# Attention, experts and a second FFN on one core: w_out's loads move to ACT's queue, stage one's operands are requested and summed at other places, two small steps are reordered

## The chip, the cores and the metric

The kernel runs on one core of a Trainium2 chip. The metric is the device time of one execution in microseconds (us); lower is better. The engines named below are PE (TensorE), DVE (VectorE), ACT (ScalarE), POOL (GpSimd) and SP (SyncE, which here only issues transfers). "PEld" is the loading of PE's weights.

## The reference

Three layers follow one another; `x` and `state` go in, 2304 rows of 512 numbers come out.

```python
def reference(**kw):
    attn_out = _attn_ref(x, state)              # 4 x 8 heads, 512 + 32 rows each, 64 wide
    x = attn_out.transpose(0, 2, 1, 3).reshape(2304 - 128, 512)   # rows of one token
    x = _moe_ref(x=x, **moe)                    # top-1 of 8 experts: relu(x @ w1[e]) @ w2[e], gated, capped
    return _moe2_ref(x=x, **moe2)
def _moe2_ref(x, w_in, w_out):
    h = x @ w_in                                # 512 -> 2048
    g = h * np.clip(h + 3.0, 0.0, 6.0) / 6.0
    return (g @ w_out).astype(np.float32)       # 2048 -> 512
```

## The kernel before, in words

After the attention (to about 73 us) come the experts: tiles of 256 tokens, one expert each, numbered s. For a tile, `xt` transposes the gathered rows on PE (L765) and splits them into a high part (ACT, L759) and a low part (DVE, L760). `gate` computes the gate's weight (DVE L775 to L782, ACT L778), `row` spreads it over the partitions (PE L788, ACT L789). Then `m1` (L797) and `m2` (L808) multiply by the expert's weights. Every float32 product is three matmuls of split halves (high by high, low by high, high by low). A tile whose expert differs from that of the tile ahead enters a branch (`tc.If`, `split`) in which its weights are split; all engines that have work in it evaluate the branch.

The **middle stage** (`mm3`, L1125, 264.5 to 440.7 us) is the first product of the second FFN: 7 chunks c of 256 tokens by 16 column blocks m. A block is 12 matmuls of 128x256 into one of eight PSUM banks taken in turn; ACT computes u (L1107), DVE g (L1108; four buffers of g), and SP writes g into `g_all` in DRAM (L1135). In the shadow of chunks 1 and later a generator, `wo_make`, prepares w_out a step at a time: `out_load` (L937) fetches half a block of w_out (512 KB, tile `st`, two buffers), DVE joins its 64-bit words into float32 (`bits`, L924, L926, L928, tile `wsrc`), POOL forms four differences (L1278), ACT and DVE split them (L1289, L1291). Blocks 6 and 7 are made first and put away in DRAM by four writes each (`wo_d`, L1298, on SP); `wo_back` (L1305, on POOL) fetches them during the next stage. In the steps of a block the load of each half stands one half ahead of its use.

The last product, g by w_out, uses Strassen and Winograd's seven products (`PRODS`) of 2 by 2 blocks. In **stage one** (L1469, 440.6 to 478.0 us) all seven sums of chunk 0 grow side by side over eight inner blocks, here called pairs j = 0 to 7; each takes 21 matmuls. For each j, `a_load(j)` brings four quarter tiles of g from `g_all` by two transfers of 128 KB on SP (L1338), `a_make(j)` forms four sums of 128x128 on POOL (L1343) and then calls `parts`: a cast on ACT (L1328) and a subtraction on DVE (L1329). The raw tiles come from a ring of six slots. Chunks 1 to 6 follow (L1489) with 128x1024 sums on POOL (L1399).

Each engine works through its own instructions in the order in which the code calls them; SP, ACT and POOL issue transfers in that same order.

Of the kernel before, what the change touches and what calls it, by code (L numbers as in the profile page):

```python
# [594 lines left out]
def full(ctx, tc, x, state, w_gate, w1, w2, capacity, w_in, w_out, out, dbg=None):  # L595
    nc = tc.nc
    V, A, G, T = nc.vector, nc.scalar, nc.gpsimd, nc.tensor
# [118 lines left out]
    w64o = w_out.bitcast(I32)  # L716
# [20 lines left out]
    def loads(which, fl, pool=None, tag=None):  # L737
        return {k: load(which, fl[1], k, fl[0], pool=pool, tag=tag) for k in (0, 2, 1, 3)}
# [8 lines left out]
    def split(which, raws, pool=(1,)):  # L747
        for k in (0, 2, 1, 3):
            split1(which, k, raws[k], pool)
# [184 lines left out]

    def out_load(m):
        st = cv.tile([128, 1024], I32, name="st")
        nc.sync.dma_start(out=st, in_=w64o[128 * m:128 * m + 128, :])  # L937
        return st

    def vload(m):  # L940
# [49 lines left out]
    def gate(xg, n=2):  # L990
        idt = ew.tile([128, 2], F32, name="idt", bufs=5)
        return idt, gate_into(xg, ew.tile([128, 2, E], F32, name="lg"), ew.tile([128, 2, 2], F32, name="mx", bufs=4), idt, n)

    def row(gv):
        gB = ew.tile([128, 256], F32, name="gB", bufs=1)
        gate_row(pT.tile([128, 256], F32, name="pgb", tag="T"), gv, gB)
        return gB

    def xt(xg):
        xT = [ew.tile([128, 4, 256], F32R, name=f"xt{h}", bufs=1) for h in "hl"]  # L1000
        for t in range(2):
            xt_into(xg[:, t], p3.tile([128, 512], F32, name="pxt", tag="3"), *(v[:, :, 128 * t:128 * t + 128] for v in xT))
        return xT
# [146 lines left out]
    vload(0)  # L1150
    vload(1)
    ids, gBs = {}, {}
    xT = {N0: xt(xg[N0])}
    ids[N0], gv = gate(xg.pop(N0))
    with tc.If(fl[N0][0] != 0):  # L1155
        split(0, r0.pop(N0))
    r1[N0] = loads(1, fl[N0])
    ft, pr, pe, pg, pid, pth, py = {}, {}, {}, {}, {}, {}, {}
    pend = sorted(PAIRS.items())
# [15 lines left out]
    for s in range(N0, NF):  # L1175
        last = s + 1 == NF
        p, n = PAIRS.get(s), PAIRS.get(s + 1)
        if p is not None:
            hp = p_m1(pth.pop(p), pr.pop(p))
            pr[p] = p_loads(1, pe[p], range(4))  # L1180

        def after0():
            with tc.If(fl[s][0] != 0):
                split(1, r1.pop(s))
            if last:
                ft[0] = fetch_c(0)
            else:
                r0[s + 1] = loads(0, fl[s + 1])
            if s == N0:
                gBs[s] = row(gv)  # L1190
            for q in [q for q in py if py[q] is not None]:
                p_y(py[q], pid[q][0], slice(256 * NF + 128 * q, 256 * NF + 128 * q + 128))
                py[q] = None

        def after1():
            if last:
                prep(0)
                for t in range(2):
                    ft[0][1](t)
                ft[1] = fetch_c(1)  # L1200
            steps(1)

        def between():
            if not last:
                ids[s + 1], gvs[0] = gate(xg.pop(s + 1))
            if n is not None:
                pid[n] = gate(pg.pop(n), 1)
            steps(1)
            if last:
                prep(2)  # L1210

        gvs = [None]
        hT = m1(xT.pop(s), {0: after0, 1: after1})
        if last:
            for t in range(2):
                ft[1][1](t)
            prep(1)
        else:
            xT[s + 1] = xt(xg[s + 1])
            if n is not None:  # L1220
                pth[n] = p_xt(pg[n])
            if s + 2 < NF:
                xg[s + 2] = gather(lrow(s + 2))
            with tc.If(fl[s + 1][0] != 0):
                split(0, r0.pop(s + 1))
            r1[s + 1] = loads(1, fl[s + 1])
            if s + 2 < NF:
                fl[s + 2] = flags(s + 2)
        if p is not None:
            hp = p_ht(hp)  # L1230
        m2(hT, ids.pop(s), gBs.pop(s), slice(256 * s, 256 * s + 256), between)
        if not last:
            gBs[s + 1] = row(gvs[0])
        steps(1)
        if p is not None:
            py[p] = p_m2(hp, pr.pop(p), pid[p][1])
        if pend and pend[0][0] == s + 2:
            p_begin()
# [87 lines left out]
    def parts(a):  # L1326
        hi, lo = htile(), htile()
        A.copy(hi, a)  # L1328
        V.tensor_tensor(out=lo, in0=a, in1=hi.bitcast(F32), op=ALU.subtract)  # L1329
        return hi, lo  # L1330
# [3 lines left out]
    def a_load(j):  # L1334
        AO[j] = a = rtile()
        for h in range(2):
            m = 8 * h + j
            nc.sync.dma_start(out=a[:, 2 * h:2 * h + 2].rearrange("p n j -> p (n j)"), in_=g_all[0:128, 256 * m:256 * m + 256])  # L1338

    def a_make(j):  # L1340
        a = AO[j]
        for o, x, z, op in ((4, 1, 3, ALU.add), (6, 0, 1, ALU.subtract), (5, 4, 0, ALU.subtract), (7, 2, 5, ALU.subtract)):
            G.tensor_tensor(out=a[:, o], in0=a[:, x], in1=a[:, z], op=op)  # L1343
        AO[j] = parts(a)


    PRODS = ((3, 6), (0, 0), (4, 3), (6, 5), (5, 4), (2, 1), (7, 2))
# [82 lines left out]
    for c in range(NCS):  # L1430
        for m in range(0 if c else 2, 16):
            if c == 0 and m in (2, 4, 6):
                r = slice(3 * m - 6, min(3 * m, 17))
                nc.sync.dma_start(out=out.rearrange("(p r) d -> p r d", r=17)[:, r], in_=zt[:, 0:DM].unsqueeze(1).broadcast_to([128, r.stop - r.start, DM]))
            mm3(m, c)
            if c == 0:
                advance(2)
                if m < 7:
                    prep(m + 1)
            else:  # L1440
                next(wg_, None)
                if m % 5:
                    next(wg_, None)
            if 0 < c < NCS - 1:
                if m == 2:
                    ft[c + 1] = fetch_c(c + 1)
                if m in (7, 10):
                    ft[c + 1][1](m // 8)
            if c == NCS - 1:
                if m == 7:  # L1450
                    a_load(0)
                    a_load(1)
                if m in (9, 11):
                    a_make(m // 2 - 4)
    for _ in wg_:
        pass

# [3 lines left out]
    fids = [ft[c][0][2] for c in range(NCS)]  # L1461
    acc = [bank(n) for n in range(7)]
    for j in range(8):
        if j + 2 < 8:
            a_load(j + 2)
        hl = AO.pop(j)
        for (x, z), ps in zip(PRODS, acc):
            for n, (l, r) in enumerate(SPLIT):
                T.matmul(ps, hl[l][:, x], WO[j][z][r], start=j == 0 and n == 0, stop=j == 7 and n == 2)  # L1469
        if j + 2 < 8:  # L1470
            a_make(j + 2)
        if NWA + j < 8:
            wo_back(NWA + j)
        if j > 2:
            q_step(1, j - 4)
# [132 lines left out]
```

## Time and profile before

| | us |
|---|---|
| median of 3 runs | 606.24 (605.2 to 608.19) |
| the profiled execution | 608.2 |
| its span in the trace | 606.2 |
| PE busy in the span | 554.9 (92%) |
| DVE, ACT, POOL busy | 365.8, 233.1, 216.9 |

The span is the time from the first to the last recorded instruction; 2.0 us of the execution lie outside it. Busy time of PE is the union of its matmuls; the time in which no matmul runs is 51.3 us.

### The profile page before, as it was taken

The page shows a single profiled execution, that of the slowest core. Times are in us where ns is not written, and L with a number is a line of the kernel's source. Part 1 is how long each engine was busy: PE and PEld are TensorE (multiplying, and loading weights), DVE is VectorE, ACT ScalarE, POOL GpSimd, SP SyncE. Part 2 cuts the span into 40 slices and gives each one's busy share as a digit, 9 for nine tenths or more (in the row PEclk, how much of TensorE's full clock was granted, in tenths as well). Part 3 has the DMA queues.
Part 4 walks back from the last instruction along what each step waited for, and adds up shares of the span by engine and source line. Part 5 has one row for each costly group of instructions (what it writes and reads, how often), then busy time and mean ns, then how long its engine had stood idle before and what let it go on. Part 6 is the DMA issues. An engine that isn't in the chain of part 4 may idle for free. (4 is left out here: it accounts for less than half of the span.)

```text
span 606.2 us, 12079 instructions
## 1 busy us (share of the span) xinstructions
PE 554.9 (92%) x4478; PEld 507.0 (84%) x4478; DVE 365.8 (60%) x730; ACT 233.1 (38%) x416; POOL 216.9 (36%) x257
## 2 busy tenths in 40 slices
PE   6997898999999999999988798999967899999995
PEld 3665688886968696999988798999966799999995
DVE  5888884355625573563454667665233958878851
ACT  4877640143214150434333444445332534433320
POOL 4436434110501010026101212220247668587841
PEclk9999799799999999999999799999989799999998
DMA  6744612989789774248676574653378334543410
GB/s 138 165 169 161 236 57 79 328 318 303 268 284 359 256 268 140 89 161 308 212 259 217 192 222 144 200 159 130 97 221 282 104 105 139 157 128 120 134 57 29
DMA packets 97906, 112.08 MB, mean 185 GB/s; under 512 B 25809, under 2 KB 74961, under 8 KB 97330
## 3 DMA queue, kind: packets, MB, share of 16 engines
q1 hardware_dynamic: 94178, 100.13, 51.0%
q0 software_dynamic: 3392, 11.05, 5.3%
q8 instruction: 37, 0.61, 0.4%
q14 instruction: 27, 0.22, 0.1%
q10 hardware_dynamic: 272, 0.07, 0.0%
HBM read 89.10 MB, written 34.84 MB: 204 GB/s over the span
## 5 line engine op out<-in xcount | busy, mean ns | idle before, releaser
L1125 PE MATMUL p<-yTh,wh 128*128 128x256 f32 x448 | 114.4, 288 | 9.0 <-DVE g L1108 7.2
L1329 DVE TENSOR_TENSOR ga<-ga 128x1024 fp32r<-128x1024 f32 x50 | 90.5, 1829 | 44.3 <-ACT ga L1328 44.2
L1125 PE MATMUL p<-yTl,wh 128*128 128x256 f32 x448 | 113.4, 283 | 2.0 <-DVE yTl L912 2.0
L1125 PEld LDWEIGHTS p<-yTh,wh 128*128 128x128 f32 x448 | 85.2, 190 | 10.0 <-DVE g L1108 7.8
L1125 PEld LDWEIGHTS p<-yTl,wh 128*128 128x128 f32 x448 | 85.8, 192 | 2.6 <-DVE yTl L912 2.6
L1328 ACT CAST ga<-ga 128x1024 fp32r<-128x1024 f32 x50 | 51.8, 1048 | 87.9 <-POOL ga L1399 34.5
L1107 ACT ACTIVATE u<-p,b 128x256 f32<-128x256 f32 x110 | 51.0, 474 | 81.2 <-DVE g L1108 52.1
L1125 PE MATMUL p<-yTh,wl 128*128 128x256 f32 x448 | 72.1, 283 | 0.0
L1399 POOL TENSOR_TENSOR ga<-ga 128x1024 f32<-128x1024 f32 x24 | 64.4, 2706 | 10.9 <-DMA ga<-g_all 10.7
L1108 DVE SCALAR_TENSOR_TENSOR g<-u,p 128x256 f32<-128x256 f32 x110 | 44.4, 416 | 34.9 <-ACT u L1107 24.5
L1125 PEld LDWEIGHTS p<-yTh,wl 128*128 128x128 f32 x448 | 61.9, 190 | 0.0
L797 PE MATMUL pm<-xth,w1h 128*128 128x256 f32 x160 | 47.0, 294 | 3.8 <-ACTq L1155 3.8
L797 PE MATMUL pm<-xth,w1l 128*128 128x256 f32 x160 | 46.2, 289 | 0.0
L797 PE MATMUL pm<-xtl,w1h 128*128 128x256 f32 x160 | 46.1, 288 | 0.0
L808 PE MATMUL pm<-hth,w2h 128*128 128x256 f32 x160 | 45.1, 282 | 0.2
L808 PE MATMUL pm<-hth,w2l 128*128 128x256 f32 x160 | 44.8, 280 | 0.0
L808 PE MATMUL pm<-htl,w2h 128*128 128x256 f32 x160 | 44.7, 279 | 0.0
L800 DVE SCALAR_TENSOR_TENSOR htl<-pm,hth 128x512 fp32r<-128x512 f32 x20 | 13.5, 687 | 46.7 <-ACT hth L799 23.7
L797 PEld LDWEIGHTS pm<-xth,w1h 128*128 128x128 f32 x160 | 31.2, 195 | 7.3 <-ACTq L1155 4.0
L1278 POOL TENSOR_TENSOR wt<-wsrc 128x256 f32<-128x256 f32 x16 | 13.1, 816 | 64.6 <-DVE wsrc L928 57.5
L1355 POOL DMA_INDIRECT out_dram<-o,fid x14 | 22.5, 1610 | 35.2 <-issue 14.5
L962 POOL TENSOR_TENSOR wl<-v,wh 128x1024 fp32r<-128x1024 f32 x6 | 15.0, 2530 | 49.1 <-ACT wh L961 49.1
(448 smaller groups left out, 1447.7 us busy)
## 6 DMA issues: line engine op xcount, KB each, us to landing
raw<-in_moe_w_dram SPq DMA_DIRECT2D x80, 512.0 KB
g_all<-g SPq DMA_DIRECT2D x110, 128.0 KB
ga<-g_all SPq DMA_DIRECT2D x24, 512.0 KB
st<-in_moe_w_in_dram SPq DMA_DIRECT2D x16, 512.0 KB
st<-in_moe_w_out_dram SPq DMA_DIRECT2D x16, 512.0 KB
x_rows<-xrow SPq DMA_DIRECT2D x4, 1072.0 KB
xb<-in_x_dram SPq DMA_DIRECT2D x32, 128.0 KB
yg<-y_pad SPq DMA_DIRECT2D x14, 258.0 KB
```

The source lines that it names most:

```text
L797: T.matmul(ps[:, j], W1[l][k][:, ls], xT[r][:, k], start=k == 0 and i == 0, stop=k == 3 and i == 2)
L800: V.scalar_tensor_tensor(out=hl, in0=ps, scalar=0.0, in1=hh.bitcast(F32), op0=ALU.max, op1=ALU.subtract)
L808: T.matmul(ps[:, j], W2[l][k // 2][:, k % 2, ls], hT[k // 2][r][:, k % 2], start=k == 0 and i == 0, stop=k == 7 and i == 2)
L962: (V if j in (0, 2) else G).tensor_tensor(out=wl, in0=v, in1=wh.bitcast(F32), op=ALU.subtract)
L1107: A.activation(out=u, in_=ps, func=AF.Relu, bias=b3)
L1108: V.scalar_tensor_tensor(out=g, in0=u, scalar=6.0, in1=ps, op0=ALU.min, op1=ALU.mult)
L1125: T.matmul(pv, l[:, 512 * q + 128 * k:512 * q + 128 * k + 128], r[:, :, 128 * k:128 * k + 128], start=n == 0, stop=n == 11)
L1278: G.tensor_tensor(out=t[:, o], in0=x, in1=z, op=ALU.subtract)
L1328: A.copy(hi, a)
L1329: V.tensor_tensor(out=lo, in0=a, in1=hi.bitcast(F32), op=ALU.subtract)
L1355: G.indirect_dma_start(out=out, out_offset=bass.IndirectOffsetOnAxis(ap=fid[:, t:t + 1], axis=0), in_=o, in_offset=None, bounds_check=B * ...
L1399: G.tensor_tensor(out=QS[c, o], in0=QS[c, x], in1=QS[c, z], op=op)
```

## The change

It has four parts. (1) `out_load` issues its 16 transfers on ACT's queue instead of SP's. (2) For the first tile of the experts' loop, the branch that splits its weights stands ahead of the tile's transposes and gate instead of behind them. (3) `row` of each later tile moves from the end of the `m2` ahead of it into its own `m1`, after the first quarter (`after0`). (4) In stage one the loads of pairs 0 to 3 are requested at m = 7, 8, 9, 10 of the last chunk (before: pairs 0 and 1, both at m = 7); `a_make` is cut into `a_sums` and `a_parts`; the sums of pairs 3 and 4 are formed on DVE, the others on POOL as before; and for each j the load of pair j + 4, the parts of j + 2 and the sums of j + 3 are called ahead of j's matmuls (before: the load of j + 2 ahead, sums and parts of j + 2 behind).

```diff
     def out_load(m):
         st = cv.tile([128, 1024], I32, name="st")
-        nc.sync.dma_start(out=st, in_=w64o[128 * m:128 * m + 128, :])
+        nc.scalar.dma_start(out=st, in_=w64o[128 * m:128 * m + 128, :])
         return st
...
-    xT = {N0: xt(xg[N0])}
-    ids[N0], gv = gate(xg.pop(N0))
     with tc.If(fl[N0][0] != 0):
         split(0, r0.pop(N0))
+    xT = {N0: xt(xg[N0])}
+    gvs = {}
+    ids[N0], gvs[N0] = gate(xg.pop(N0))
...
-            if s == N0:
-                gBs[s] = row(gv)
+            gBs[s] = row(gvs.pop(s))
...
-        if not last:
-            gBs[s + 1] = row(gvs[0])
...
-    def a_make(j):
-        a = AO[j]
+    def a_sums(j):
+        a, eng = AO[j], V if j in (3, 4) else G
         for o, x, z, op in ((4, 1, 3, ALU.add), (6, 0, 1, ALU.subtract), (5, 4, 0, ALU.subtract), (7, 2, 5, ALU.subtract)):
-            G.tensor_tensor(out=a[:, o], in0=a[:, x], in1=a[:, z], op=op)
-        AO[j] = parts(a)
+            eng.tensor_tensor(out=a[:, o], in0=a[:, x], in1=a[:, z], op=op)
+
+    def a_parts(j):
+        AO[j] = parts(AO[j])
...
             if c == NCS - 1:
-                if m == 7:
-                    a_load(0)
-                    a_load(1)
-                if m in (9, 11):
-                    a_make(m // 2 - 4)
+                if m in (7, 8, 9, 10):
+                    a_load(m - 7)
+                if m in (9, 11, 13):
+                    a_sums(m // 2 - 4)
+                if m in (10, 12):
+                    a_parts(m // 2 - 5)
...
     for j in range(8):
+        if j + 4 < 8:
+            a_load(j + 4)
         if j + 2 < 8:
-            a_load(j + 2)
+            a_parts(j + 2)
+        if j + 3 < 8:
+            a_sums(j + 3)
         hl = AO.pop(j)
         for (x, z), ps in zip(PRODS, acc):
             for n, (l, r) in enumerate(SPLIT):
                 T.matmul(ps, hl[l][:, x], WO[j][z][r], start=j == 0 and n == 0, stop=j == 7 and n == 2)
-        if j + 2 < 8:
-            a_make(j + 2)
```

Lines of the kernel after shift by up to three: its L1335 is L1338 of before, L1340 is L1343, L1326 is L1329, L1286 is L1289.

PE's order at the start of the experts' loop, as a difference (L1155 and L1153 are the same branch, L765 are the first tile's transposes):

```order
+L1153 COMPARE_AND_BRANCH
+L1153 UNCONDITIONAL_BRANCH x2
 L765 MATMUL pxt<-identk,xg 128x128 x8
-L1155 COMPARE_AND_BRANCH
-L1155 UNCONDITIONAL_BRANCH x2
 L797 MATMUL pm_1785<-xth,w1h_93 128x256
```

The branch now stands ahead of the transposes, and the same on ACT, DVE and POOL.

SP's queue of before in the middle stage, where the first block of w_out is put away and the loads of the next one follow:

```order
L1135 DMA g_all<-g 128x256 x7
L1298 DMA wo_d<-wo6h 128x1024
L1298 DMA wo_d<-wo6l 128x1024
L1298 DMA wo_d<-wo6bh 128x768
L1298 DMA wo_d<-wo6bl 128x768
L937 DMA st<-in_moe_w_out_dram 128x1024
L1135 DMA g_all<-g 128x256 x2
L937 DMA st<-in_moe_w_out_dram 128x1024
```

ACT's order of the change at the same place (L1286 are casts of w_out, L1107 the activations of blocks, L911 the cast of the next chunk):

```order
L1286 CAST wo6bh<-wsrc 128x512
L1107 ACTIVATE u<-p_4180,b_82 128x256
L937 DMA st<-in_moe_w_out_dram 128x1024
L1107 ACTIVATE u<-p_4207,b_82 128x256
L911 CAST yTh_4046<-yg 128x512
L1107 ACTIVATE u<-p_4229,b_82 128x256
L937 DMA st<-in_moe_w_out_dram 128x1024
L1107 ACTIVATE u<-p_4251,b_82 128x256
```

The two loads no longer stand behind the four writes of `wo_d`, nor behind writes of g; they stand between activations, and the writes stay on SP.

DVE's order of the change in stage one (L1326 are the subtractions of `parts`, L1340 the sums of `a_sums`):

```order
L1326 TENSOR_TENSOR ga<-ga 128x1024
L1340 TENSOR_TENSOR ga<-ga 128x128 x4
L1326 TENSOR_TENSOR ga<-ga 128x1024
L1340 TENSOR_TENSOR ga<-ga 128x128 x4
L1326 TENSOR_TENSOR ga<-ga 128x1024 x7
```

They are, in turn, the low part of pair 2, the sums of 3, the low part of 3, the sums of 4, and then the low parts of 4 to 7 and of chunk 1's first operands. Before, DVE had nine subtractions in a row here and no sum; on POOL the twelve sums that stay behind `wo_back`'s issues are now those of pairs 5, 6 and 7 alone.

SP's order of the change at the same place (L1394 are chunk 1's loads):

```order
L1335 DMA ga<-g_all 128x256 x2
L1135 DMA g_all<-g 128x256 x5
L1335 DMA ga<-g_all 128x256 x8
L1394 DMA ga<-g_all 128x8x128 x24
```

The first row is the load of pair 3; the five writes are those of the last blocks of g, and the loads of pairs 4 to 7 stand right behind them. Before, the loads of pairs 2 to 5 stood behind the last eight writes, and those of 6 and 7 behind loads of chunk 1.

## Rows read from the trace of the kernel before

**Rows 1.** Page, part 1: engine, busy us (share of the span) xinstructions.
```profile
PE 554.9 (92%) x4478; PEld 507.0 (84%) x4478; DVE 365.8 (60%) x730; ACT 233.1 (38%) x416; POOL 216.9 (36%) x257
```

**Rows 2.** Windows table: stretch, length, busy us of each engine, clock, DMA share, GB/s.
```profile
300.00:350.00 50.00, 42.37 (x330) 41.40 (x329) 26.96 (x60) 18.72 (x39) 9.29 (x12) 0.93 0.66 228
...
350.00:400.00 50.00, 46.59 (x385) 45.99 (x384) 33.35 (x74) 23.78 (x50) 11.55 (x15) 1.00 0.55 176
...
440.00:478.00 38.00, 26.95 (x177) 24.73 (x176) 16.98 (x14) 13.54 (x17) 24.76 (x35) 0.87 0.64 201
...
478.00:599.00 121.00, 119.74 (x1008) 119.37 (x1007) 89.73 (x88) 40.53 (x43) 78.00 (x34) 1.00 0.41 120
```

**Rows 3.** Timeline of PE: start, length, instruction, [idle before it <- releaser].
```profile
107.47 0.58 PE L797 MATMUL pm<-xth,w1h 128*128 128x256 f32 x1 [3.80 <-ACTq L1155]
...
136.88 0.43 PE L788 MATMUL pgb<-identk,mx 128*128 128x128 f32 x2 [0.72 <-DVE lg L775]
...
318.25 0.39 PE L1125 MATMUL p<-yTh,wh 128*128 128x256 f32 x1 [1.83 <-DVE g L1108]
...
337.08 0.58 PE L1125 MATMUL p<-yTh,wh 128*128 128x256 f32 x1 [5.14 <-DVE g L1108]
...
471.23 0.58 PE L1469 MATMUL po<-wo7h,ga 128*128 128x256 f32 x1 [2.42 <-ACT ga L1328]
```

**Rows 4.** Timeline of DVE at the first tile of the experts.
```profile
105.34 1.29 DVE L760 TENSOR_TENSOR xtl<-pxt,xth 128x512 fp32r<-128x512 f32 x2 [0.43 <-DVE xb L812]
```

**Rows 5.** Waits: engine, tile, line <- releaser: us in total, times, longest.
```profile
DVE wsrc L924 <- DMA st<-in_moe_w_out_dram: 29.0, 8, 7.2
...
DVE g L1108 <- DMA g_all<-g: 10.3, 5, 5.0
```

**Rows 6.** Timeline of SP's queue in the middle stage.
```profile
310.39 1.02 SPq L937 DMA_DIRECT2D st<-in_moe_w_out_dram  x1
...
328.87 1.33 SPq L937 DMA_DIRECT2D st<-in_moe_w_out_dram  x1
```

**Rows 7.** Timeline of ACT in the middle stage.
```profile
305.07 0.48 ACT L1107 ACTIVATE u<-p,b 128x256 f32<-128x256 f32 x1
...
324.52 0.84 ACT L1107 ACTIVATE u<-p,b 128x256 f32<-128x256 f32 x2 [0.47 <-DVE g L1108]
```

**Rows 8.** Timeline of DVE in the middle stage.
```profile
316.71 0.43 DVE L924 TENSOR_SCALAR wsrc<-st 128x512 int32<-128x512 int32 x1 [6.76 <-DMA st<-in_moe_w_out_dram]
...
335.55 0.43 DVE L924 TENSOR_SCALAR wsrc<-st 128x512 int32<-128x512 int32 x1 [7.17 <-DMA st<-in_moe_w_out_dram]
```

**Rows 9.** Timeline of POOL in stage one.
```profile
447.14 1.81 POOL L1343 TENSOR_TENSOR ga<-ga 128x128 f32<-128x128 f32 x4 [7.65 <-DMA ga<-g_all]
...
455.29 7.53 POOL L1343 TENSOR_TENSOR ga<-ga 128x128 f32<-128x128 f32 x12
...
468.29 1.81 POOL L1343 TENSOR_TENSOR ga<-ga 128x128 f32<-128x128 f32 x4 [3.10 <-DMA ga<-g_all]
```

**Rows 10.** Timeline of SP's queue around stage one.
```profile
444.12 3.74 SPq L1338 DMA_DIRECT2D ga<-g_all  x8
...
462.53 0.92 SPq L1338 DMA_DIRECT2D ga<-g_all  x2
```

**Rows 11.** Page, part 5: costliest groups, busy us, mean ns of one.
```profile
L1328 ACT CAST ga<-ga 128x1024 fp32r<-128x1024 f32 x50 | 51.8, 1048 | 87.9 <-POOL ga L1399 34.5
...
L1108 DVE SCALAR_TENSOR_TENSOR g<-u,p 128x256 f32<-128x256 f32 x110 | 44.4, 416 | 34.9 <-ACT u L1107 24.5
```

**Rows 12.** Timeline of DVE in stage one.
```profile
437.95 1.23 DVE L1329 TENSOR_TENSOR ga<-ga 128x1024 fp32r<-128x1024 f32 x1 [4.89 <-ACT ga L1328]
...
442.76 0.79 DVE L1108 SCALAR_TENSOR_TENSOR g<-u,p 128x256 f32<-128x256 f32 x2 [0.27 <-ACT u L1107]
...
463.93 2.34 DVE L1329 TENSOR_TENSOR ga<-ga 128x1024 fp32r<-128x1024 f32 x1 [1.43 <-ACT ga L1328]
```

**Rows 13.** DMA issues: transfer, queue, count, KB each, median us to landing.
```profile
wo6bh<-wo_d POOLq DMA_DIRECT2D x1, 384.0 KB, 8.9
```

More of the change, by code (lines that the diff above doesn't have):

```diff
@@ L1204, in between @@
             if not last:
-                ids[s + 1], gvs[0] = gate(xg.pop(s + 1))
+                ids[s + 1], gvs[s + 1] = gate(xg.pop(s + 1))
             if n is not None:
@@ L1210, in between @@
                 prep(2)
-        gvs = [None]
         hT = m1(xT.pop(s), {0: after0, 1: after1})
```

## The prediction

> **What bounds the kernel now.** The page's first part comes first: PE is busy for 554.9 of 606.2 us [rows 1], so 51.3 us without a matmul are what a change of order can win; no other engine is near its limit. The table of windows says where they lie. In the last stretch, 478 to 599 us, 1008 matmuls take 119.74 us of busy PE, 0.1188 us each, at a granted clock of 1.00 [rows 2]. At that pace 50 us hold 421 matmuls; the stretch 300 to 350 has 330, so 91 are missing, or 10.8 us. Its idle time is 50 - 42.37 = 7.6 us; the other 3.2 us are matmuls run at the lower of the clock's two levels, 1.2 instead of 2.4 GHz; the mean clock of 0.93 shows them, in a stretch whose other feature is that PE stood idle. The stretch 350 to 400 misses 36 matmuls, 4.3 us. Stage one (440 to 478) misses 320 - 177 = 143, or 17.0 us: 11.0 idle, 6.0 at the lower clock (mean 0.87). So 32 of the losses lie in the stretches that the change touches. The timeline of PE names what ended the waits: in the middle stage DVE's g (1.83 and 5.14 us), in stage one the operands' parts, at the start of the experts the branch (3.80), and at 136.88 the gate's row (0.72) [rows 3].
>
> **Start and rows.** Before, PE sat 3.80 us until the branch (the wait that ended last is ACT's queue at L1155) and began at 107.47. With the branch ahead, what PE needs is xtl, and DVE has it at 105.34 + 1.29 = 106.63 [rows 4]. That is 0.8 us earlier; I take 0.6, since the branch itself still costs something where it now stands. Bounds: 0 if the branch costs as much ahead of the transposes, and 1.5 if PE can start on the first half of xtl. The moved `row` removes the wait of 0.72 at the second tile; a quarter of `m1` (24 matmuls, 2.9 us) now covers the gate's last steps on DVE and ACT. I take 0.7, bounds 0 and 1. Together **1.3 us**.
>
> **w_out's loads.** DVE waits 29.0 us in eight waits for `st` [rows 5]; the two longest are 6.76 (to 316.71) and 7.17 (to 335.55) [rows 8]. Everything behind the waiting conversion on DVE is late by it: the g of the blocks, so the PSUM banks, so PE once its lead of eight banks (11.4 us at 1.43 a block) is used up; that is where 1.83 and 5.14 come from. The two late loads are issued by SP at 310.39 and 328.87 [rows 6], each just behind four writes of w_out. On ACT the first stands behind the activation that began at 305.07, so at about 305.6, the second behind the first of the pair begun at 324.52, so at about 325 [rows 7]: 4.8 and 3.9 us earlier, and now ahead of the writes' bytes on the transfer engines instead of behind them. The transfers took 316.71 - 310.39 = 6.3 and 6.7 us from issue to use. If they take as long again, the waits shrink to about 2.0 and 3.3; as they run ahead of the writes, I expect less. A wait of 2 to 3 us is below PE's lead, so all of 1.83 goes and of 5.14 at least 3.9. With the idle time goes most of the lower clock behind it. Of the 10.8 us lost in 300 to 350 I count 9 back, of the 4.3 in 350 to 400, where DVE's waits for `st` are short and the load is issued at about the same time by either engine, 1. **10 us**; bounds 5 (the second wait keeps its transfer time and the clock stays low behind it) and 14 (nearly all of 15.1).
>
> The cost of it: sixteen issues on ACT between activations, at most the 1.33 us that the longer of SP's took [rows 6], 21 us in all. ACT is busy 18.72 of 50 us there [rows 2], so they lie beside PE. The second load of each pair also waits on ACT until DVE has converted the tile that lies in its buffer; behind it stand the activations, and behind those g and PE. DVE's conversion stands just ahead, so I expect a hold of about 1 us, covered by the lead of eight banks.
>
> **Stage one.** 168 matmuls at 0.1188 are 20.0 us; the stage took 37. Before, only pairs 0 and 1 were ready; the loads of 2 to 5 stood behind the last eight writes of g and were issued at 444.12 [rows 10], POOL's first sum came at 447.14 [rows 9], and every pair then paid in turn: four sums on POOL (1.81 alone, 7.53 / 3 = 2.51 in the row of twelve), a cast of 1.05 [rows 11] and a subtraction of 1.23 [rows 12], with eight issues of `wo_back` among the sums. The last load went out at 462.53, once a ring slot was free, and was used at 468.29, 5.76 us later [rows 9, 10]; PE waited 2.42 for that pair's cast alone [rows 3].
>
> Now I count from T, the start of the stage, with 2.49 us a pair. Pairs 0 to 3 are loaded 7 to 13 us before T, the sums of 0 to 2 and the parts of 0 and 1 done in the last blocks. The parts of 2 stand behind the last u on ACT and the last g on DVE. Before, the last g ended at 442.76 + 0.79 = 443.55 [rows 12], 3 us into the stage; now DVE has no other work ahead of it, so I take T + 2.5, the cast from about T + 2 to 3.1, the subtraction to T + 4.3; wanted at 5.0. The four sums on DVE are not in the trace. Between 128x256 (0.416, [rows 11]) and 128x1024 (1.23) the slope is 1.06 ns a column, so 128x128 would be 0.28, four of them 1.1 us; bounds: 4 x 0.416 = 1.7 above, and below 4 x (1.23 / 8) = 0.6. I take 1.1. Pair 3: T + 4.3, sums 1.1, cast 1.05, subtraction 1.23: T + 7.7, wanted at 7.5. Pair 4's load is issued behind the last writes of g, about T + 4.4; it is used 3.0 us later if it goes like that of 444.12, 5.8 if like that of 462.53. Then 3.4 us of sums, cast and subtraction: T + 10.8 to 13.6, wanted at 10.2, so PE waits 0.6 to 3.4. For 5 to 7 POOL needs at most 2.51 us each and PE 2.49, so nothing grows from there. `wo_back`'s eight transfers can be issued within the stage's first 5 us, without sums between them, and land 8.9 us later [rows 13], by T + 14; wanted from T + 15 on. With one or two us at the lower clock the stage takes 22 to 26 us. Of 17.0 lost I count 13 back: **13 us**; bounds 6 and 16.
>
> DVE's sums also meet POOL's. The row at 463.93 shows a subtraction of 2.34 beside a POOL sum of 128x1024, that of 437.95 one of 1.23 beside POOL's sums of 128x128 [rows 12]; so beside small sums I add nothing. The Trainium skill ("SBUF — State Buffer", the section on SBUF's two separate sides) has a DVE operation with two SBUF inputs and a GpSimd operation that reads SBUF lock one shared port pair, the second standing still for the whole of the first. The row of 463.93 agrees, that of 437.95 does not show it; by the rule each of DVE's eight sums could wait for one of POOL's, some 0.5 us each by [rows 9], and the sum here would be 21 instead of 24.
>
> **The sum.** 1.3 + 10 + 13 = 24.3 us. From the profiled execution's 608.2 (span 606.2 and 2.0 around it) that gives 583.9; it lies 2.0 above the median of 606.24, from which it gives 581.9. I predict **583**.
>
> **The rivals.** (a) The w_out loads land no sooner: only the issue moves, while the transfer engines are full with the same writes, so DVE waits until the same time. For it: 6.3 and 6.7 us from issue to use at both places, much above the 3.0 of the load at 444.12. Against it: the new issue lies ahead of the writes. Then 14.3 us are won: 592 to 594. The Trainium skill ("DMA: Bandwidth & Descriptors", the section that issuing engines are not separate DMA queues) speaks for this rival: transfers of all engines run on the same 16 engines, and another issuer saves only the issuing. By that rule rival (a) is the forecast; here the issue itself stood behind other issues, which is what its saving is. (b) Stage one stays bound by transfers: the loads of 4 to 7 now run beside both of `wo_back`'s groups, and take the 8.9 us of those [rows 13] instead of 3 to 6. Pair 4 then comes 4 to 6 us later: 587 to 590. (c) Writes of g land late behind `wo_d`'s, and g's four buffers run out; DVE waited 10.3 us for them in all [rows 5]. It would keep half of the middle stage's gain: 588. (d) Slower: ACT, holding a w_out load until its buffer is free, holds the activations. In eight blocks each hold beyond PE's lead costs PE the rest. To use up 24 us of gains it would have to exceed the lead by 3 us in each of eight blocks; at 4.5 us the time is 618. Against it: the conversion it waits for is always just ahead on DVE. (e) Nothing happens, because the waits are ended by other things: PE's waits are named plainly, so little speaks for it.
>
> **Chances.** The forecast (578 to 588) 0.50; (a) 0.15; (b) 0.15; (c) 0.06; (a) with (b), 596 to 600, 0.05; more than forecast, 570 to 578, 0.03; (d) 0.03; (e) 0.03. The range 575 to 595 holds the forecast, (a), (b) and (c), 8 to 9 in 10. Half a per cent, 3 us, is about what a measurement of this kernel tells from no change: faster 0.94, same 0.03, slower 0.03.
>
> **What would show it.** Right: at the place of 318.25 and 337.08 PE has no wait over 1 us, and DVE's sum of waits for `st` falls from 29.0 to under 18; the clock of the middle stage is 1.00 throughout; stage one's length falls to 22 to 26 us with one wait of 1 to 4 us, at pair 4; the first `m1` begins 0.6 us after xtl's end at the latest. Wrong: if DVE waits as long for `st`, step two failed; if PE waits at several pairs of stage one, step three; if ACT's activations stand behind the loads for over 3 us, rival (d) has begun.

## The result, and the profile after

The changed kernel takes 589.7 us (median of 4 runs, 589.24 to 589.93) against 605.88 for the kernel before (now a median of 4): ratio 0.9726, 95% interval 0.9699 to 0.9752. That is 16 us faster; the prediction was 583 with a range of 575 to 595. The profiled execution took 589.24 us, its span is 587.5. Between the two profiled spans lie 18.7 us, since that of before was 2.3 us above its median and that of after 0.5 below.

The windows after, with the columns of [rows 2] (length, busy time and instructions of each engine, clock, DMA share, GB/s); the last is stage one:

```profile
300.00:350.00 50.00, 47.69 (x393) 47.08 (x393) 33.12 (x73) 21.66 (x45) 9.74 (x13) 1.00 0.77 258
350.00:400.00 50.00, 50.00 (x419) 49.98 (x418) 37.44 (x81) 25.57 (x53) 11.53 (x15) 1.00 0.56 180
425.00:457.00 32.00, 23.25 (x169) 22.55 (x167) 15.58 (x19) 10.89 (x14) 19.76 (x24) 0.84 0.69 213
```

In 300 to 350 us there are now 393 matmuls where there were 330, at a clock of 1.00 instead of 0.93; 350 to 400 has 419, two short of the 421 that fit at full pace. Stage one still idles 8.75 of 32 us, at a clock of 0.84.

The timeline of PE after, with the waits and the first instruction of each stage:

```profile
103.69 0.39 PE L797 MATMUL pm<-xth,w1h 128*128 128x256 f32 x1 [0.86 <-ACT xth L759]
105.50 0.58 PE L797 MATMUL pm<-xtl,w1h 128*128 128x256 f32 x1 [1.43 <-DVE xtl L760]
...
260.44 0.28 PE L1125 MATMUL p<-yTh,wh 128*128 128x256 f32 x1
...
331.34 0.38 PE L1125 MATMUL p<-yTh,wh 128*128 128x256 f32 x1 [0.89 <-ACT yTh L911]
...
424.61 0.28 PE L1473 MATMUL po<-wo0h,ga 128*128 128x256 f32 x1
...
442.95 0.58 PE L1473 MATMUL po<-wo4h,ga 128*128 128x256 f32 x1 [7.19 <-ACT ga L1325]
...
456.81 0.28 PE L1491 MATMUL po<-wo0h,ga 128*128 128x256 f32 x1
...
462.26 0.39 PE L1491 MATMUL po<-wo0bh,ga 128*128 128x256 f32 x1 [1.89 <-DVE yg L1366]
```

Set beside the starts of before (264.5, 440.6 and 477.8 us), the stages begin at 260.44, 424.61 and 456.81. So the start gave 4.1 us, the middle stage went from 176.0 to 164.2 (11.9 won), stage one from 37.2 to 32.2 (5.0 won), and the six chunks from 121.2 to 123.8 (2.6 lost). With 0.3 behind the last chunk that is the 18.7. Of [rows 3], the wait of 3.80 is now 0.86 and 1.43, and 0.72, 1.83 and 5.14 are gone; a wait of 7.19 us at pair 4 is new, and one of 1.89 at chunk 1. The start's 4.1 us is one sample: in the nine other traces with the same start (all runs below but undo_branch, undo_row and undo_start) the middle stage begins between 259.99 and 263.18 us, 1.4 to 4.5 us before the 264.54 of before.

Behind the first tile's waits the clock differs too. The stretch of 110 to 115 us before and after:

```profile
110.00:115.00 5.00, 5.00 (x33) 5.00 (x33) 0.69 (x1) 0.97 (x2) 0.30 (x1) 0.72 1.01 336
...
110.00:115.00 5.00, 5.00 (x45) 5.00 (x44) 1.97 (x4) 1.56 (x3) 0.00 (x0) 1.00 1.03 373
```

PE is busy throughout in both, but after the wait of 3.80 us it gets through 33 matmuls at a mean granted clock of 0.72, after 0.86 and 1.43 through 45 at 1.00. Twelve matmuls are 1.4 us.

DVE's waits after, against [rows 5]:

```profile
DVE g L1108 <- DMA g_all<-g: 17.8, 7, 5.6
...
DVE ga L1340 <- DMA ga<-g_all: 8.5, 1, 8.5
...
DVE wsrc L924 <- DMA st<-in_moe_w_out_dram: 4.8, 3, 3.3
```

Its waits for `st` fell from 29.0 to 4.8 us. Those for the landing of g rose from 10.3 to 17.8, and pair 4's sums wait 8.5.

ACT's queue and casts in the middle stage (L937 are the loads that stood on SP):

```profile
299.22 0.33 ACTq L937 DMA_DIRECT2D st<-in_moe_w_out_dram  x1
...
314.81 0.33 ACTq L937 DMA_DIRECT2D st<-in_moe_w_out_dram  x1
...
327.22 0.62 ACT L911 CAST yTh<-yg 128x512 fp32r<-128x512 f32 x1 [6.18 <-DMA yg<-y_pad]
...
373.59 0.34 ACTq L937 DMA_DIRECT2D st<-in_moe_w_out_dram  x1
374.03 0.84 ACT L1107 ACTIVATE u<-p,b 128x256 f32<-128x256 f32 x2 [3.18 <-DVE wsrc L928]
```

SP's queue:

```profile
318.30 1.05 SPq L1295 DMA_DIRECT2D wo_d<-wo7bl  x1
319.40 2.39 SPq L905 DMA_DIRECT2D yg<-y_pad  x2
...
423.60 4.00 SPq L1135 DMA_DIRECT2D g_all<-g  x5
431.76 6.10 SPq L1335 DMA_DIRECT2D ga<-g_all  x8
```

ACT issues the two loads that were late at 299.22 and 314.81, each in 0.33 us. That is 1 to 3 us ahead of SP's four writes of `wo_d` in their turn, the last of which is the row of 318.30, where before they stood behind these. Counted from the start of the middle stage they go out 7.1 and 10.0 us earlier than before, and they are used 5.0 and 4.1 us after their issue instead of 6.3 and 6.7: most of the gain is the earlier issue, the rest the shorter transfer. What is left of the middle stage's loss is the row of 327.22: the cast of the next chunk's tokens waits 6.18 us for their transfer, which SP issues at 319.40 behind the same writes; PE loses 2.3 us by it at 328.8 to 332.6 (0.89 of them in the row of 331.34).

The last two ACT rows show a cost. From the third load on, every other one goes out only when DVE has converted the tile that lies in its buffer, and the next activation stands behind it on ACT. In all seven such places that activation starts later than its block on PE, its buffer of u and ACT's own work would have let it, by 1.1 us at the least, about 1.8 mostly, and 3.1 at 374.03. PE shows no wait there, so its lead covers these holds.

Then stage one: POOL's timeline, DVE's, and the windows of three stretches in it:

```profile
426.17 0.60 POOL L1302 DMA_DIRECT2D wo6h<-wo_d  x1
...
429.94 0.59 POOL L1302 DMA_DIRECT2D wo7bl<-wo_d  x1
...
446.65 1.32 POOL L1340 TENSOR_TENSOR ga<-ga 128x128 f32<-128x128 f32 x1
```

```profile
428.92 1.01 DVE L1340 TENSOR_TENSOR ga<-ga 128x128 f32<-128x128 f32 x4
...
440.80 1.02 DVE L1340 TENSOR_TENSOR ga<-ga 128x128 f32<-128x128 f32 x4 [8.53 <-DMA ga<-g_all]
...
446.43 1.23 DVE L1326 TENSOR_TENSOR ga<-ga 128x1024 fp32r<-128x1024 f32 x1 [1.96 <-ACT ga L1325]
...
451.74 10.14 DVE L1326 TENSOR_TENSOR ga<-ga 128x1024 fp32r<-128x1024 f32 x4 [1.43 <-ACT ga L1325]
461.80 0.87 DVE L1366 SCALAR_TENSOR_TENSOR yg<-po,yg 128x256 f32<-128x256 f32 x2
```

```profile
432.00:436.00 4.00, 3.77 (x32) 3.56 (x30) 0.27 (x1) 0.00 (x0) 0.00 (x0) 1.00 1.14 404
436.00:440.00 4.00, 0.00 (x0) 0.00 (x0) 0.00 (x0) 0.00 (x0) 0.00 (x0) 0.98 1.13 376
...
444.00:448.00 4.00, 3.47 (x16) 3.48 (x17) 1.70 (x2) 1.05 (x1) 3.84 (x7) 0.50 0.41 104
```

SP's waits for that load and two others of stage one (us in total, times, longest):

```profile
SPq L1335 <- DMA g_all<-g: 5.4, 3, 3.6
```

With no sums between them, `wo_back`'s eight transfers (3.6 MB) leave POOL's queue from 426.17 to 430.5, from 1.6 us into the stage on. In the two stretches of 432 to 440 us the transfer engines move 404 and 376 GB/s. SP has issued its last writes of g by 427.6 and then stands until 431.76 before it can issue the load of pair 4; 3.6 us of that it waits for writes of g to land, since the pair's ring slot lies in memory that g's last buffers held. The sums of that pair begin at 440.80, 9.0 us after the issue. PE waits 7.19 for the cast and 0.77 for the subtraction, and behind that the granted clock is 0.50, the lower of its two levels: 16 matmuls in 444 to 448 us.

### The profile page after: what moved, and what is told of

Its sections match the earlier page's. It is cut to its first block, busy times and chain, and to the rows that moved or that the text cites. A ratio compares the mean times of both kernels' runs of the same rounds, so it can differ in the third digit from the quotient of the medians.

```text
span 587.5 us, 12092 instructions
## 1 busy us (share of the span) xinstructions
PE 550.0 (94%) x4478; PEld 504.5 (86%) x4478; DVE 380.3 (65%) x738; ACT 233.4 (40%) x416; POOL 212.2 (36%) x249
## 5 line engine op out<-in xcount | busy, mean ns | idle before, releaser
L1326 DVE TENSOR_TENSOR ga<-ga 128x1024 fp32r<-128x1024 f32 x50 | 101.6, 2058 | 20.0 <-ACT ga L1325 20.0
L1125 PE MATMUL p<-yTh,wh 128*128 128x256 f32 x448 | 112.5, 284 | 1.5 <-ACT yTh L911 0.9
L1125 PE MATMUL p<-yTl,wh 128*128 128x256 f32 x448 | 112.1, 281 | 0.8 <-DVE yTl L912 0.8
L1125 PEld LDWEIGHTS p<-yTl,wh 128*128 128x128 f32 x448 | 84.5, 189 | 1.0 <-DVE yTl L912 1.0
L1107 ACT ACTIVATE u<-p,b 128x256 f32<-128x256 f32 x110 | 51.1, 474 | 65.9 <-DVE g L1108 29.4
L1354 POOL DMA_INDIRECT out_dram<-o,fid x14 | 20.2, 1443 | 39.1 <-DVE o L1366 21.3
```

Source lines behind the costliest of these rows:

```text
L1107: A.activation(out=u, in_=ps, func=AF.Relu, bias=b3)
L1125: T.matmul(pv, l[:, 512 * q + 128 * k:512 * q + 128 * k + 128], r[:, :, 128 * k:128 * k + 128], start=n == 0, stop=n == 11)
L1354: G.indirect_dma_start(out=out, out_offset=bass.IndirectOffsetOnAxis(ap=fid[:, t:t + 1], axis=0), in_=o, in_offset=None, bounds_check=B * ...
```

## The experiments

Every kernel below is the changed kernel with one edit. Each time is a median with its ratio to the kernel before run beside it.

**w_out's loads back on SP's queue (undo_queue).**

```diff
-        nc.scalar.dma_start(out=st, in_=w64o[128 * m:128 * m + 128, :])
+        nc.sync.dma_start(out=st, in_=w64o[128 * m:128 * m + 128, :])
```

> The change with w_out's loads back on SP's queue. Theory: the middle stage (L1125) goes back from 164.3 to about 175 us, DVE's waits for st from 4.8 to 25 us or more, PE's waits of 1.8 and 5.1 us return; time 600 to 602. Rival (a) of the prediction, that the issuing queue hardly matters and the gain came from elsewhere: middle stage 165 to 168, time 590 to 593.

600.8 us, 0.9919 (0.9892 to 0.9947). Its waits, and the timeline of PE:

```profile
DVE wsrc L924 <- DMA st<-in_moe_w_out_dram: 28.8, 8, 7.6
```

```profile
314.21 0.39 PE L1125 MATMUL p<-yTh,wh 128*128 128x256 f32 x1 [1.31 <-DVE g L1108]
...
333.49 0.58 PE L1125 MATMUL p<-yTh,wh 128*128 128x256 f32 x1 [5.58 <-DVE g L1108]
```

The old waits are back at the same places, the middle stage takes 176.0 us again. The queue alone is worth 11 us, and rival (a) falls: the same bytes to the same buffers land in time when another engine issues them. On SP the two stand behind the four writes, and behind writes of g that wait for DVE, and go out 6.5 and 9.5 us later in the stage than in the changed kernel; from issue to use they then take 6.4 and 7.1 us, against 5.0 and 4.1.

**The branch, the row, and both undone (undo_branch, undo_row, undo_start).**

Of the three, undo_branch is the first piece, undo_row the two behind it, undo_start all.

```diff
+    xT = {N0: xt(xg[N0])}
+    gvs = {}
+    ids[N0], gvs[N0] = gate(xg.pop(N0))
     with tc.If(fl[N0][0] != 0):
         split(0, r0.pop(N0))
-    xT = {N0: xt(xg[N0])}
-    gvs = {}
-    ids[N0], gvs[N0] = gate(xg.pop(N0))
...
-            gBs[s] = row(gvs.pop(s))
+            if s == N0:
+                gBs[s] = row(gvs.pop(s))
...
+        if not last:
+            gBs[s + 1] = row(gvs.pop(s + 1))
```

> The change with its second part undone (the first tile's branch behind its transposes and gate again). Theory: the middle stage began 4.1 us earlier in the changed kernel, of which the branch made about 2.5 (a wait of 3.80 turned into 0.86 + 1.43, and about 1 us less at the lower clock behind it): 591.5 to 593. Rival (the forecast's own size): 0.6 us, 590 to 590.5.

> The change with its third part undone (each later tile's row at the end of the m2 ahead of it). Theory: the wait of 0.72 us at the second tile returns and nothing else: 590 to 590.7. Rival: the moved row also made the rest of the 4.1 us at the start, 1.5 us or more: above 591.

> The change with its second and third part undone together. Theory, after the runs with one of them undone (592.4 and 595.1): the branch alone makes PE reach the second tile's row earlier, where the gate then holds it 4 us and the clock falls, so that the branch without the moved row is worth nothing or a loss; without both the start is that of the kernel before, 4.1 us later: 593 to 594.5, that is at or below the 595.1 with only the row undone. Rival (the two parts add up): 589.7 + 2.7 + 5.4 = 597 to 598.

592.43 (0.9764, 0.9720 to 0.9808), 595.14 (0.9804, 0.9751 to 0.9856) and 593.18 us (0.9755, 0.9725 to 0.9786). The branch came out as expected, and so did both together; the row did not: leaving it where it was costs 5.4 us, more than leaving both. Three views of that run, in turn the timeline of PE, that of DVE, and the windows:

```profile
136.08 0.69 PE L788 MATMUL pgb<-identk,mx 128*128 128x128 f32 x2 [3.97 <-DVE lg L775]
```

```profile
131.76 2.32 DVE L745 TENSOR_TENSOR w1l<-raw,w1h 128x1024 fp32r<-128x1024 f32 x1 [1.32 <-ACT w1h L744]
...
134.60 0.16 DVE L775 TENSOR_TENSOR lg<-xg 128x16 f32<-128x16 f32 x1
```

```profile
135.00:140.00 5.00, 3.92 (x10) 1.30 (x12) 4.25 (x18) 0.57 (x3) 0.00 (x0) 0.52 0.84 293
140.00:145.00 5.00, 5.00 (x22) 1.57 (x20) 1.54 (x3) 0.23 (x1) 0.00 (x0) 0.79 0.89 266
```

With the branch moved, PE is done with the first tile's `m2` 3.6 us earlier than with both undone (at 132.11 instead of 135.68). But the gate stands on DVE behind the splitting of weights for the next tile, and that ends at about the same time as ever (134.08; 134.31 to 134.87 in the kernel before, the changed one and the one with both undone). So PE waits 3.97 us for the row instead of 0.72, and behind the wait the mean granted clock is 0.52 and 0.79 in the next two stretches of 5 us. In the changed kernel the row stands behind a quarter of `m1`, and no such wait is there. The runs of each of the three spread by 2 to 3 us and their intervals overlap, so that the branch without the row is worse than neither rests on the traces (3.97 and 1.02 us of wait; the middle stage begins at 266.85 and 264.29) more than on 595.1 against 593.2.

**No `wo_back` transfers (wb_off).** Blocks 6 and 7 of w_out are not fetched; PE multiplies by blocks 0 and 1 in their place.

```diff
-                nc.gpsimd.dma_start(out=w.rearrange("p n c -> p (n c)"), in_=wo_d[...])
-        WO[j] = wo_views(tt, bb)
+                pass
+        WO[j] = WO[j - NWA]
```

> The change without wo_back's eight transfers: blocks 6 and 7 of w_out are not fetched, PE multiplies by blocks 0 and 1 in their place. Theory (traffic): pair 4's operands are late because these 3.6 MB are now issued in one go at the start of stage one; without them pair 4's load is issued by 6 us into the stage and used about 3 us later, PE waits 0 to 3 us for it instead of 8, the stage takes 21 to 25 us instead of 32.2. Rival (slot): the load waits on SP for its ring slot whatever the traffic; it is issued 7 us into the stage as now, PE waits 4 us, stage 26 to 28. Rival (sums on DVE): nothing changes, 32.

578.43 us, one run. SP's queue, DVE and PE in stage one:

```profile
428.74 3.73 SPq L1335 DMA_DIRECT2D ga<-g_all  x8
```

```profile
432.38 1.15 DVE L1340 TENSOR_TENSOR ga<-ga 128x128 f32<-128x128 f32 x4
```

```profile
444.73 0.39 PE L1473 MATMUL po<-wo1h,ga 128*128 128x256 f32 x1 [1.03 <-DVE ga L1326]
```

The load of pair 4 goes out at 428.74, 4.4 us into the stage, and DVE forms its sums at 432.38 without a wait, 3.6 us later. PE's one wait for operands is 1.03 us at pair 7; the stage takes 22.8 us (424.32 to 447.10). Slot and sums are those of the changed kernel, so the traffic it is (sums_pool below, where half of it goes out later, lies in between): it held the issue of pair 4's load back by 2.7 us (the writes of g that it waits for land late) and the load itself by 5.4.

**Stage one undone (undo_stage).** Loads, sums and parts stand where they stood before.

```diff
-                if m in (7, 8, 9, 10):
-                    a_load(m - 7)
+                if m == 7:
+                    a_load(0)
+                    a_load(1)
...
-        if j + 4 < 8:
-            a_load(j + 4)
+        if j + 2 < 8:
+            a_load(j + 2)
```

> The change with its fourth part undone (stage one's loads, sums and parts stand where they stood before); parts one to three stay. Theory: in the changed kernel stage one gained 5.0 us (37.2 to 32.2) and the chunks behind it lost 2.6 (121.2 to 123.8), so undoing it costs 1 to 5 us: 591 to 595. Rival, the fourth part is worth what the prediction gave it, 13 us, and something else lost the rest: 600 or more. Rival, it is worth nothing: 589 to 590.

591.57 us (588.62 to 593.89; 0.9769, 0.9734 to 0.9805). The fourth part is worth about 2 us, not 13, and as the intervals of this run and of the changed kernel overlap, the times alone don't tell the 2 from nothing; in this run stage one takes 35.1 us and the chunks 122.3, together 1.3 more than in the changed kernel.

**All sums on POOL (sums_pool).**

```diff
-        a, eng = AO[j], V if j in (3, 4) else G
+        a, eng = AO[j], G
```

> The change with the sums of pairs 3 and 4 on POOL instead of DVE. Theory (traffic): pair 4's operands are late by their load, so the engine of the sums hardly counts; but POOL's sums of pair 3 now stand behind nothing but wo_back's issues: if they stand ahead of these, wo_back starts about 2 us later and stage one changes by under 2 us, time 588 to 591. Rival (sums on DVE were the point of part four): pair 3 is late by 2 to 3 us and pair 4 by 1 more: 592 to 594. Rival (DVE's sums hurt): under 587.

586.72 us, 0.9694 (0.9641 to 0.9747): not slower than with the sums on DVE, and in the range of the last expectation, that DVE's sums hurt. SP's timeline, POOL's and PE's:

```profile
428.29 4.22 SPq L1335 DMA_DIRECT2D ga<-g_all  x8
```

```profile
427.69 0.60 POOL L1302 DMA_DIRECT2D wo6h<-wo_d  x1
...
435.07 1.81 POOL L1340 TENSOR_TENSOR ga<-ga 128x128 f32<-128x128 f32 x4 [5.14 <-issue]
436.82 0.56 POOL L1302 DMA_DIRECT2D wo7h<-wo_d  x1
```

```profile
438.01 0.39 PE L1473 MATMUL po<-wo4h,ga 128*128 128x256 f32 x1 [2.48 <-ACT ga L1325]
...
458.90 0.58 PE L1491 MATMUL po<-wo0bh,ga 128*128 128x256 f32 x1 [4.07 <-DVE yg L1366]
```

POOL now issues block 6 alone at 427.69 and block 7 behind pair 4's sums at 436.82; PE's wait at pair 4 is 2.48 and stage one takes 27.1 us. The trace gives the traffic as the reason, and not DVE's sums, of which no cost is shown: pair 4's load goes out at 428.29, 4.4 us into the stage, and its sums begin 6.8 us later, with one block of `wo_back` on the way. Without `wo_back` that was 3.6 us, with both blocks 9.0. But at chunk 1 PE waits 4.07 instead of 1.89.

**Pairs 4 and 5 in the first two slots (ring).**

```diff
-    rings = {"r": [(rw, "raw0", 4)] * 4 + [(None, "gr", 2)] * 2,
+    rings = {"r": [(rw, "raw0", 4)] * 6 + [(None, "gr", 2)] * 2,
...
+                if m in (13, 15):
+                    a_load(m // 2 - 2)
...
-        if j + 4 < 8:
-            a_load(j + 4)
+        if j == 0:
+            for i in range(6, 8):
+                a_load(i)
```

> The change with the ring of raw tiles reordered so that pairs 4 and 5 take the first two slots again, and their loads requested at m = 13 and 15 of the last chunk, ahead of wo_back's traffic; pairs 6 and 7 are loaded at the start of stage one. Theory (traffic): pairs 4 and 5 are ready in time, PE's 8 us at pair 4 go; pairs 6 and 7, still loaded beside wo_back, come 0 to 3 us late; stage one 22 to 26 us, time 580 to 585. Rival: something else than the traffic of these loads holds the stage, it stays over 29 us and the time over 587.

588.05 us, 0.971 (0.9654 to 0.9765); stage one 30.6. PE, and POOL at pair 5's sums:

```profile
437.21 0.39 PE L1476 MATMUL po<-wo4h,ga 128*128 128x256 f32 x1 [0.67 <-ACT ga L1325]
...
445.40 0.58 PE L1476 MATMUL po<-wo5h,ga 128*128 128x256 f32 x1 [4.39 <-ACT ga L1325]
```

```profile
442.47 1.80 POOL L1340 TENSOR_TENSOR ga<-ga 128x128 f32<-128x128 f32 x4 [11.16 <-DMA ga<-g_all]
```

The wait moved from pair 4 (0.67) to pair 5 (4.39). The loads called at m = 13 and 15 stand on SP behind writes of g that wait for DVE: pair 4's goes out at 427.45, just behind the first of `wo_back`'s transfers (426.95), pair 5's at 429.84, among the last of them, and its sums wait for it until 442.47, 12.6 us. Stage and time are those of the rival (over 29 and over 587), but its reason isn't: what holds pair 5 is its load beside the same traffic.

**`wo_back` behind the loads (wb_sp), and with A22 first (best3).** Loads 4 to 7 are issued together, `wo_back` on SP's queue behind them.

```diff
-        if j + 4 < 8:
-            a_load(j + 4)
+        if j == 0:
+            for i in range(4, 8):
+                a_load(i)
...
-                nc.gpsimd.dma_start(out=w.rearrange("p n c -> p (n c)"), in_=wo_d[...])
+                nc.sync.dma_start(out=w.rearrange("p n c -> p (n c)").bitcast(F32), in_=wo_d[...])
 # best3 also
-            q_load(d, ("A21", "A22"))
+            q_load(d, ("A22", "A21"))
```

> The change with the loads of pairs 4 to 7 issued together and wo_back's transfers behind them on SP's queue instead of POOL's. Theory (traffic): pair 4's wait shrinks from 8 to 0 to 3 us; w_out's block 7 may now be a little late (0 to 2 us); stage one 22 to 27 us, time 581 to 586. Rival (slot): pair 4 is still issued 7 us into the stage and used 3 later, wait 4: 27 to 29, time 585 to 588. Rival (sums on DVE): 589 to 591.

> The run with wo_back behind the loads on SP's queue (586.3), with chunk 1's operand A22 loaded ahead of A21 instead of behind it. Theory: PE's 2.5 + 1.9 us at chunk 1's start, for A22's parts, shrink by about 1.3 us, the time of the other load's 512 KB at 400 GB/s, and less time is lost to the lower clock behind them: 583 to 585.5, stage one as in that run (23 us). Rival: the transfers that stage one needs fill the engines until 20 us into it in any order, and the time stays at 585.5 to 588.

586.28 us, 0.9687 (0.9620 to 0.9755), and 586.28, 0.9656 (0.9619 to 0.9693). PE in the first, and in the second:

```profile
450.52 0.39 PE L1492 MATMUL po<-wo0h,ga 128*128 128x256 f32 x1 [2.50 <-ACT ga L1325]
```

```profile
458.70 0.39 PE L1492 MATMUL po<-wo0bh,ga 128*128 128x256 f32 x1 [4.10 <-DVE yg L1366]
```

Stage one takes 23.0 and 23.7 us, counted up to the wait for chunk 1's first operand, as the prediction had it for the change itself. Then chunk 1 pays: its operands, now last in the queue, are late (PE waits 2.50 and 1.94); with A22 first that is 0.68 and 0.76, but the wait for a PSUM bank grows from 1.88 to 4.10. So stage one is as the theories had it, and both times lie in the rivals' ranges.

**The next chunk's tokens requested at m = 0 (best1 on wb_sp with chunk 1's loads between blocks 6 and 7; best2 on sums_pool).**

```diff
-                if m == 2:
+                if m == 0:
                     ft[c + 1] = fetch_c(c + 1)
...
```

> The run with wo_back behind the loads on SP's queue, with chunk 1's first two operands loaded between blocks 6 and 7 of w_out (in that run they came 8 us late behind both), and the tokens of the next chunk requested at m = 0 instead of 2 (ahead of the writes of wo_d). Theory: stage one 23 to 26 us, no wait over 1.5 us at chunk 1's start, PE's 2 us at the yTh of chunk 3 gone; 576 to 582. Rival: with all transfers in one stretch some operand is always late, block 7 now by 3 us or more: 583 to 587.

> The change with all sums on POOL, as in the earlier run (586.7), and the tokens of the next chunk requested at m = 0. Theory: only PE's 2 us at the yTh of chunk 3 go, stage one as in that run (27 us): 583.5 to 585.5. Rival: the tokens' transfers still land late behind the writes, nothing changes: 586 to 588.

585.54 us, 0.9663 (0.9615 to 0.9712), and 590.75, 0.9735 (0.9712 to 0.9757). In best1 block 7 is late by 2.62 + 0.84 us and more, as its rival had it; its time is in that rival's range. In best2 the first half of the tokens was cast at 324.2 us, and PE waited at the same place all the same. DVE's timeline:

```profile
330.56 0.42 DVE L1108 SCALAR_TENSOR_TENSOR g<-u,p 128x256 f32<-128x256 f32 x1 [5.86 <-DMA g_all<-g]
```

Now g waits 5.86 us for one of its four buffers, whose write to `g_all` lands late behind `wo_d`'s. This is rival (c) of the prediction, with 2 us of PE's time to it. best2 is 4 us above sums_pool; its first tile lost 2 us by the time of 123 us, which the edit doesn't touch (its waits there are 1.30 and 1.61 instead of 0.86 and 1.43, and the granted clock of 110 to 115 us is 0.71 instead of 1.00), and the rest is open. Its time lies above both expectations.

## Why the prediction was right in its range and wrong in its terms

**w_out's loads: right.** 10 us were forecast, 11.9 measured (11.1 between the medians with the queue undone). DVE's waits for `st` fell to 4.8 us where under 18 was named, and the clock of the middle stage is 1.00. What rival (d) is made of is there: seven activations stand behind a load for 1.1 to 3.1 us, where about 1 was expected and over 3 was named as its sign (one is just over). But PE's lead covered them, as forecast. The residue is of the kind of rival (c): other transfers (tokens, g) behind the same writes, 2.3 us.

**Start and rows: the mechanism right in part, the size off.** 1.3 us was forecast, 4.1 measured, about 3 in the mean of the traces with this start. The term was worked out as two separate waits, 0.6 and 0.72. The first left out two things: PE begins on the high part (103.69), before the low part xtl is there, and behind the shorter waits the clock stays up, which is worth 1.4 us in 110 to 115 us; with the branch back (undo_branch) that stretch has 35 matmuls at 0.74. The runs also showed that the two belong together: the branch's gain arrives at the row, whose time DVE sets, and would have turned into a wait of 3.97 us and a lower clock. The moved row is worth not the 0.72 us that it showed in the profile of before but what the earlier edit would have made of it.

**Stage one: wrong, and the step that failed** is "it is used 3.0 us later if it goes like that of 444.12, 5.8 if like that of 462.53". It went out 2.8 us later than forecast (7.2 instead of 4.4 into the stage), as writes of g landed late, and was used 9.0 us after that. Both bounds came from rows in which `wo_back` was spread by sums on POOL; that the change takes these sums from between its issues was said in the same paragraph, as help for `wo_back`, and its traffic was not set against the loads. Rival (b), at 0.15, had it: 8.9 us for the load, and 587 to 590; the forecast proper, 578 to 588, at 0.50, was missed. Without the traffic the stage takes 22.8 us (wb_off), with the loads ahead of it 23.0 (wb_sp), so the 22 to 26 us of the forecast exist, but only with `wo_back` out of the way, which the change did not do. Of the 13 us, 8.0 went to pair 4's wait; behind it the lower clock cost 3.2 (169 matmuls took 23.25 us where 0.1188 each are 20.1), and one or two had been counted. A further 2.6 were lost in the chunks.

**The range held in part by luck.** The start and the loads gave 4.7 us more than was counted, which pays for over half of the 8 that stage one fell short, and the chunks' 2.6 stood in no term.

**What was not in the prediction** is chunk 1's start. At 451.74 four of DVE's subtractions stand in a row, pair 7's and the first three for chunk 1's operands. Beside POOL's 128x1024 sums three of them take 2.34, 3.42 and 3.40 us, the fourth, alone, 1.21: 10.14 in all. The `yg` that frees the bank stands behind them at 461.80, and PE waits 1.89. With stage one faster it stays or grows: 4.07 in sums_pool, 4.10 in best3. The row of 463.93 [rows 12] had shown the doubling; its place behind stage one was not looked at. The Trainium skill ("SBUF — State Buffer", the section on SBUF's two separate sides) states an exclusive lock between such a pair of operations; the rows of 128x1024 fit it.

The small sums fit it too, and there the forecast read its row wrongly: DVE's subtraction of 437.95 stays at 1.23, but the sum of 128x128 that POOL began beside it, at 438.17, took 1.33 us instead of 0.46. It is the one that starts second that waits. In the changed kernel POOL's sum of 446.65 takes 1.32 beside the subtraction of 446.43, and the like happens beside those of pairs 4 and 6 (1.43 and 1.33). The twelve sums of pairs 5 to 7 take 8.10 us, 2.70 a pair, where at most 2.51 was counted. For DVE's own small sums the forecast of 1.1 us was good (1.01 and 1.02), but both times POOL formed no sum beside them, so whether the two kinds hold each other was not seen.

**A faster version:** the four with stage one's transfers in another order (wb_sp, best1, best3, sums_pool) have ratios of 0.966 to 0.969 against the changed kernel's 0.9726; ring (0.971) and best2 (0.9735) do not differ from it. Only best3's interval (0.9619 to 0.9693) lies wholly below the changed kernel's (0.9699 to 0.9752), so it is the better by some 0.7%, as the best of six tried; the runs of the others spread by 4 to 8 us and their intervals overlap it.

What stays open: whether a version exists in which neither pair 4, block 7 nor chunk 1 waits. From 4 us into the stage 5.1 MB (loads 1.0, `wo_back` 3.6, chunk 1's first operand 0.5) have to land; at the 376 to 404 GB/s of the changed kernel's windows there, an estimate is 13 us, which ends at 17, and w_out's block 7 is wanted at 17 (seven pairs of 2.49 us).

## What to carry to other kernels

A transfer that moves to an emptier queue wins what stood ahead of it, bytes included, and holds what stands behind it on the new queue for as long as it waits for its buffer. But work taken from between two transfers on a queue lets them go earlier too, and they may then run into the loads that the change meant to speed up, so every queue's traffic is to be laid on one time axis after the change. Two waits in series on one engine have one price: the one behind shows in the profile only what the one ahead has left of it. And a stage that is freed hands its pressure to the next one's first operands, so the forecast should reach one stage further than the edit.

## What the runs showed of the hardware

The clock's price is large beside the wait that precedes it: after 3.97 us of waiting the mean granted clock was 0.52 and 0.79 in the next two stretches of 5 us, so that PE ran for part of each at the lower of its two levels (1.2 instead of 2.4 GHz), in a place where 1.02 us of waiting (the run with both start parts undone) was followed by 1.00. A pair's load of 256 KB that is used 3.6 us after its issue without `wo_back`'s 3.6 MB was used after 6.8 us beside half of them and after 9.0 us beside all, although another engine had issued these. And when DVE's subtraction and POOL's sum met, the one that began second waited: POOL's of 128x128 took 1.32 instead of 0.46 us, DVE's of 128x1024 2.34 instead of 1.23.
